# Two attention and feed-forward layers for one new token: one wo load turned on chip, split layer norm, queries turned in PSUM, an earlier gate, and one more V head kept

## The chip, the cores and the metric

The kernel runs on one core of a Trainium2 chip. A core has five engines that run their own queues of instructions side by side: TensorE (PE; its weight loads are shown apart as PEld), VectorE (DVE), ScalarE (ACT), GpSimd (POOL) and SyncE (SP), which here does little but issue loads. Loads from HBM are moved by 16 DMA engines, in the order in which SP issued them. On-chip data lies in SBUF (128 partitions), results of TensorE in PSUM (128 partitions, eight banks of 512 fp32 a partition). The metric is device time in microseconds, lower is better.

## The reference

Four tokens (B = 4), each with its own cache. Two layers share one set of weights and one cache: attention, feed-forward, attention, feed-forward, each with a layer norm in front and a residual sum behind.

```python
def _layernorm(x, axis=-1, eps=1e-5):
    m = jnp.mean(x, axis=axis, keepdims=True)
    v = jnp.var(x, axis=axis, keepdims=True)
    return (x - m) / jnp.sqrt(v + eps)
# x (4,1,512); k_cache, v_cache (4,8,4096,128); wq (512,4096); wo (4096,512); all bf16
def _A_ref(x, k_cache, v_cache, wq, wo):                # 32 query heads, 8 K/V heads, 4096 keys
    q = (x @ wq).reshape(B, Sq, 32, 128).transpose(0, 2, 1, 3)
    k, v = jnp.repeat(k_cache, 4, axis=1), jnp.repeat(v_cache, 4, axis=1)
    scores = jnp.einsum("bhqd,bhkd->bhqk", q, k) * (128 ** -0.5)
    o = jnp.einsum("bhqk,bhkd->bhqd", _softmax(scores), v)
    return o.transpose(0, 2, 1, 3).reshape(B, Sq, 4096) @ wo
def _B_ref(x, w_gate, w_up, w_down):                    # w_gate, w_up (512,1792), w_down (1792,512)
    return (gelu_tanh(x @ w_gate) * (x @ w_up)) @ w_down
x = x + _A_ref(_layernorm(x), ...); x = x + _B_ref(_layernorm(x), ...)
x = x + _A_ref(_layernorm(x), ...); x = x + _B_ref(_layernorm(x), ...)
```

## The kernel before

**Stages.** The kernel goes through the batch one element (token) at a time; "batch 0" to "batch 3" are these four. For each it does the first layer's attention, the first feed-forward and the second layer's attention. The second feed-forward is done once for all four tokens at the end. The first queries of all four tokens are computed at the start (tag "i"), the second queries batch by batch.

**Loads.** All weights stay in SBUF: wq and wo with 32 KB a partition, w_gate, w_up and w_down with 14 KB each. K and V heads of 1 MB (8 KB a partition) go into twelve slots, the tile `KV`. Eight slots hold the K heads of the current batch until the second layer's scores have read them. V turns over in the rest, and is read from HBM twice, once for each layer. `HELD[b]` (line 22) names V heads that stay in their slot from the first layer to the second and so are loaded once: none in batch 0, head 7 in the others. The second layer's V of batches 0 to 2 (`HALVES`) comes in two loads of 512 KB with 4 KB rows, into one half of a slot each. At the end the first four V heads of the second layer of batch 3 go into wq's space, once the last query products have read it.

SP issues, in this order: wq; K of batch 0; the first half of wo; V of batch 0; the second half of wo; w_gate, w_up, w_down in two halves; then for b = 1 to 3: K of batch b, V of batch b for the first layer, V of batch b - 1 for the second; last V of batch 3 for the second layer. Each issue waits on SP until the slot that it overwrites has been read, and everything behind it waits too. `ld_wo` (L794) loads wo with the 128 rows of a head on the partitions, as the products want it, in pieces of 1 KB.

**Order.** The instruction order is not written out. `Plan` (L65) holds a node for each step with an engine, a guessed duration and what it depends on; `Plan.run` lays the nodes out by a small model of the engines and of the DMA, gives each load its slot, and so fixes the order on every engine before the program is built. `LEAD`, `PATIENCE` and the `DMA_` constants (L28 to L41) steer it. `Plan.warm` fills waits of TensorE with idle products (`spin`, L1004).

**Scores.** Six of eight K heads are turned by VectorE (`turn`, L366, in place), two (5 and 7) by TensorE and ScalarE (L373, L379). `scores` (L401) needs the queries spread over the partitions: `qsplit` (L595), `qrep` (L605), `expand` (L392), in two halves z = 0 and z = 1 for K heads 0 to 3 and 4 to 7. Then maximum (L421 to L432), exponential (L438), a turn of the weights (L447 by VectorE, L455 by TensorE, L463 by ScalarE), the products with V (`values`, L485) and the scaling (L493).

**The chain between the attentions.** Output products with wo (`proj`, `proj_last`, L613 and L623), turned and added to the residual (`addback`, L646 and L647). Layer norm: squares (L500), one TensorE product that sums values and squares over the partitions (L506), sums (L512), subtraction of the mean (L513), variance (L521, L522), root by ScalarE (L529, L530); the root is applied later, in the gate or as the scale of the scores. Feed-forward: products with w_gate and w_up into two PSUM banks (L655), each turned by VectorE (`ffturn`, L662), then the gate (L678 to L707), then products with w_down in two halves (L715). The gate's two turned halves share one place in SBUF, so the second turn comes after the first one's use; in `gelu_y` and `gelu_c` the turned up half is multiplied in first, then the reciprocal is taken. Second queries (`qproj`, L829): products with wq for z = 0 and 1 (`qmm`, L538), each copied to bf16 by ScalarE (L551), turned by VectorE (L556) and spread; `qnat` (L563) makes the form that the heads turned by TensorE need.

Of the kernel before, what the change touches and what calls it, by code (L numbers as in the profile page):

```python
# [14 lines left out]
P = 128  # L15
# [6 lines left out]
HELD = ((), (7,), (7,), (7,))  # L22
HALVES = {(b, 1, j) for b in range(3) for j in range(8)} | {(3, 1, 6)}
# [7 lines left out]
DMA_FETCH = 1.5  # L31
DMA_LEAD = 4.0

PATIENCE = (0.5, 1.5, 0.7)
LEAD = {"tn1": -3, "val0": 1, "sc10": -2, "chain": 2, "sc11": -6, "sm00": 1, "os0": -6, "op": -2, "sm01": 11, "sm10": 10, "qx1": 4, "other": 5, "sc00": 2, "sm11": 8, "os1": -4, "tn0": -2, "sc01": 1}
# [3 lines left out]
FILL = 0.7  # L39
SPIN = 0.22  # L40
STREAM = {"sc": 0.85, "qm": 0.85, "up": 0.75, "up2": 0.75, "kt": 0.21, "pw": 0.16, "qp": 0.11, "qn": 0.05,  # L41
          "su": 0.02, "lnm": 0.03, "xt": 0.1, "ys": 0.2, "dn": 0.38, "dn2": 0.38}


def stage(n):
# [13 lines left out]
    if n[0] in ("lnq", "lnm", "lnc", "lnv", "lnr", "up", "ft", "ga", "gb", "gy", "gc", "zz", "dn", "da", "qm", "qe",  # L59
                "qt", "qn", "qc", "qk"):  # L60
        return "chain"
# [3 lines left out]
class Plan:  # L65
# [149 lines left out]
    def warm(self, places):  # L215
# [3 lines left out]
        for n, _ in self.order:  # L219
# [16 lines left out]
            past.append((z, last, 0.72 * d if kind == "val" else d - 0.15 if kind in ("op", "op2") else STREAM.get(kind, 0.0)))  # L236
# [4 lines left out]
def kernel(  # L241
# [261 lines left out]
    def ln_mm(bs, nb):  # L503
        def emit():
            st = R_ps[1][:, 0:2 * CD * nb].rearrange("p (s k b) -> p s k b", s=2, k=CD)
            nc.tensor.matmul(st, lhsT=ones_mean, rhs=XS[:, :, :, bs], start=True, stop=True)  # L506
        return emit

    def ln_mid(bs, nb):
        def emit():  # L510
            st = R_ps[1][:, 0:2 * CD * nb].rearrange("p (s k b) -> p s b k", s=2, k=CD)
            nc.vector.tensor_reduce(out=mu[:, :, 0:nb], in_=st, axis=AX.X, op=ALU.add)  # L512
            nc.vector.tensor_tensor(out=xn[:, :, bs], in0=XT[:, :, bs],  # L513
                                    in1=mu[:, 0, 0:nb].unsqueeze(1).broadcast_to([P, CD, nb]),
                                    op=ALU.subtract)
        return emit

    def ln_var(nb):
        def emit():
            t = lt[:, 0:nb]  # L520
# [12 lines left out]
    def qmm(z, bs, nb):  # L533
# [7 lines left out]
        return emit  # L541

# [46 lines left out]
    def qsplit(z, b):  # L589
        def emit():  # L590
            if b:
# [17 lines left out]
    def proj(src, nb, heads, first, last):  # L609
        def emit():  # L610
            for j in heads:
                for i in range(4):
                    nc.tensor.matmul(R_ps[0][32 * i:32 * i + nb, :], lhsT=src[:, 4 * j + i, 0:nb],  # L613
# [4 lines left out]
    def proj_last(src, nb, heads, last):  # L618
        def emit():
            todo = [4 * j + i for j in heads for i in range(4)]  # L620
            for h in todo:
                for t in range(4):
                    nc.tensor.matmul(R_ps[1][32 * t:32 * t + nb, 0:P], lhsT=src[:, h, 0:nb],  # L623
# [36 lines left out]
    def ffturn(z):  # L660
        def emit():
            nc.vector.transpose(out=PD[:, 0:FT].rearrange("p (c x) -> p c x", c=CF),  # L662
                                in_=R_ps[z][:, 0:FT].rearrange("p (r c) -> p c r", c=CF))
        return emit

    def ff(nb):
        n = CF * nb
        at, ah = (0, n) if nb > 1 else (992, 984)
        d = PD[:, 0:FT].rearrange("p (c x) -> p c x", c=CF)[:, :, 0:nb]
        u = PD[:, FT:FT + n].rearrange("p (c b) -> p c b", c=CF)  # L670
        g = PF[:, at:at + n].rearrange("p (c b) -> p c b", c=CF)
# [19 lines left out]
    def gelu_y(nb, y):  # L691
        def emit():
            d, g, u, h = ff(nb)
            if nb == 1:
                nc.vector.scalar_tensor_tensor(out=g, in0=g, scalar=y, in1=d, op0=ALU.mult, op1=ALU.mult)
            else:
                nc.vector.tensor_tensor(out=g, in0=g, in1=y.unsqueeze(1).broadcast_to([P, CF, nb]),
                                        op=ALU.mult)
                nc.vector.tensor_tensor(out=g, in0=g, in1=d, op=ALU.mult)
        return emit  # L700

    def gelu_c(nb):
# [349 lines left out]
```

## Time and profile before

| | us |
|---|---|
| three runs | 294.04, 294.3, 291.69 (median 294.04) |
| the profiled execution | 291.89 |
| its span in the profile | 290.1 |

The profile shows one execution. DMA moved 111.42 MB from HBM, 97.5 MB of it in 1 MB and 0.5 MB loads of K and V heads. Times in the profile are microseconds from the start of the span. "L715" is line 715 of the kernel before. Views used below: the page (engine shares, the span in 40 slices, the chain of waits that ended last, groups of instructions), windows (one row a stretch: busy time of each engine with its count of instructions, the granted clock of TensorE, the mean busy share of the DMA engines, GB/s), the timeline (instructions in order of time), and the chain of waits in order of time (start, length, what).

### The profile page before, as it was taken

The numbers are of one execution on the slowest core, as the hardware profiler recorded it, in microseconds if no ns is written. First come the engines' busy times: TensorE is split into PE (matmuls) and PEld (weight loads), VectorE is DVE, ScalarE is ACT, GpSimd is POOL, SyncE is SP. The second block draws the span as 40 slices with busy tenths as digits, with TensorE's granted clock in tenths as the row PEclk, the third lists the DMA queues.
The fourth block names the chain that finished last, engine by engine and source line by source line (L and its number), as shares of the span: only waits on it lengthen the run. The fifth ranks groups of instructions, "written<-read, shape, count | busy, mean of one in ns | idle before, by whom it ended". The sixth has DMA issues, their size and how long they took to land.

```text
span 290.1 us, 9733 instructions
## 1 busy us (share of the span) xinstructions
PE 236.3 (81%) x4419; PEld 138.3 (48%) x4419; DVE 133.5 (46%) x380; ACT 74.5 (26%) x167; POOL 0.7 (0%) x6
## 2 busy tenths in 40 slices
PE   4988887878687888798888698879977889897794
PEld 1433454443233565455434465554445655565552
DVE  4149911002289942052389721343998213444034
ACT  1020751001023852101224731000338321113010
POOL 0000000000000000000000000000000000000000
PEclk9999999999999999999999999999999999999999
DMA  7999999999999999999999999999999999999910
GB/s 312 412 421 419 376 405 416 414 371 426 415 407 395 419 421 417 402 407 406 393 417 416 425 416 411 405 407 390 413 422 416 408 387 403 396 382 420 411 47 1
DMA packets 21657, 112.04 MB, mean 386 GB/s; under 512 B 2032, under 2 KB 6128, under 8 KB 12272
## 3 DMA queue, kind: packets, MB, share of 16 engines
q1 hardware_dynamic: 21568, 111.42, 95.3%
q8 instruction: 34, 0.56, 0.8%
q14 instruction: 7, 0.06, 0.0%
q10 hardware_dynamic: 48, 0.01, 0.0%
HBM read 111.42 MB, written 0.00 MB: 384 GB/s over the span
## 4 chain that ended last, share of the span: by engine, by line
DMA 62%; PE 16%; SPq 11%; DVE 7%; issue 2%; ACT 1%; DVEq 0%
DMA KV<-in_A_v_cache_dram 43%; DMA KV<-in_A_k_cache_dram 8%; SPq L351 7%; PE O_ps L485 7%; DMA wd_sb<-in_B_w_down_dram 6%; DMA wq_sb<-in_A_v_cache_dram 5%; SPq L741 3%; PE S_ps L415 3%; DVE KV L366 2%; PE R_ps L715 1%; PE R_ps L538 1%; DVE PA L662 1%; PE S_ps L1004 1%; PE R_ps L655 1%; DVE sm L421 1%
## 5 line engine op out<-in xcount | busy, mean ns | idle before, releaser
L485 PE MATMUL O_ps<-PA,KV 128*128 128x56 bf16 x1920 | 66.3, 188 | 20.8 <-DMA KV<-in_A_v_cache_dram 17.3
L485 PEld LDWEIGHTS <-KV 128*128 128x128 bf16 x1920 | 57.6, 97 | 40.8 <-DMA KV<-in_A_v_cache_dram 32.4
L1004 PE MATMUL S_ps<-iden_b 128*128 128x512 bf16 x226 | 67.7, 401 | 3.6 <-DVE iden_b L321 3.6
L366 DVE STREAM_TRANSPOSE KV<-KV 128x1024 int32<-128x1024 int32 x48 | 56.5, 1214 | 0.6 <-DMA KV<-in_A_k_cache_dram 0.4
L379 ACT ACTIVATE KV<-R_ps 128x512 bf16<-128x512 f32 x64 | 34.9, 595 | 28.0 <-PE R_ps L373 27.9
L415 PE MATMUL S_ps<-KV,PA 128*32 128x512 bf16 x384 | 35.3, 394 | 2.1 <-DVE KV L366 1.3
L1004 PEld LDWEIGHTS <-iden_b 128*128 128x128 bf16 x227 | 21.9, 107 | 27.6 <-issue 11.7
L373 PE MATMUL R_ps<-iden_b,KV 128*128 128x128 bf16 x256 | 22.1, 219 | 6.3 <-ACT KV L379 3.1
L421 DVE TENSOR_REDUCE sm<-S_ps 128x1 f32<-128x512 f32 x16 | 10.8, 677 | 27.4 <-PE S_ps L415 27.4
L373 PEld LDWEIGHTS <-KV 128*128 128x128 bf16 x256 | 15.8, 97 | 14.8 <-issue 10.2
L415 PEld LDWEIGHTS <-PA 128*32 128x32 bf16 x384 | 11.4, 94 | 13.2 <-issue 4.4
L493 DVE TENSOR_TENSOR OT<-O_ps,XS 128x4 bf16<-128x4 f32 (+1 forms) x12 | 2.0, 164 | 32.9 <-PE O_ps L485 32.9
L415 PE MATMUL S_ps<-KV,QN 128*32 128x512 bf16 x128 | 16.8, 381 | 0.2 <-ACT KV L379 0.2
L438 ACT ACTIVATE PA<-S_ps,sm 128x512 bf16<-128x512 f32 x16 | 11.7, 732 | 20.4 <-DVE sm L432 17.6
L632 ACT ACTIVATE PA<-R_ps 128x256 f32<-128x256 f32 x10 | 3.8, 384 | 46.2 <-PE R_ps L613 41.1
L529 ACT ACTIVATE sm<-sm 128x1 f32<-128x1 f32 (+1 forms) x10 | 2.0, 203 | 52.6 <-DVE sm L522 52.6
L493 DVE TENSOR_TENSOR OT<-O_ps,rdk 128x16 bf16<-128x16 f32 (+3 forms) x18 | 3.1, 170 | 26.7 <-PE O_ps L485 26.7
L463 ACT ACTIVATE PA<-T_ps 128x512 bf16<-128x512 f32 x16 | 9.6, 597 | 13.0 <-PE T_ps L455 11.8
L556 DVE STREAM_TRANSPOSE PA<-PA 128x256 int32<-128x256 int32 x10 | 4.4, 437 | 14.9 <-ACT PA L551 14.2
L613 PE MATMUL R_ps<-wo_sb,OT 128*1 128x512 bf16 (+1 forms) x124 | 8.7, 378 | 2.6 <-DMA wo_sb<-in_A_wo_dram 1.4
L646 DVE STREAM_TRANSPOSE PA<-R_ps 128x128 f32<-128x128 f32 x9 | 2.9, 317 | 16.5 <-PE R_ps L623 10.2
L447 DVE STREAM_TRANSPOSE PA<-PA 128x256 int32<-128x256 int32 x16 | 7.0, 434 | 7.5 <-ACT PA L438 7.5
(92 smaller groups left out, 173.9 us busy)
## 6 DMA issues: line engine op xcount, KB each, us to landing
KV<-in_A_v_cache_dram SPq DMA_DIRECT2D x34, 1024.0 KB, 15.0
KV<-in_A_k_cache_dram SPq DMA_DIRECT2D x32, 1024.0 KB, 13.5
KV<-in_A_v_cache_dram SPq DMA_DIRECT2D x46, 512.0 KB, 7.0
wq_sb<-in_A_wq_dram SPq DMA_DIRECT2D x1, 4096.0 KB, 12.2
wo_sb<-in_A_wo_dram SPq DMA_DIRECT2D x2, 2048.0 KB, 19.5
wq_sb<-in_A_v_cache_dram SPq DMA_DIRECT2D x4, 1024.0 KB
wg_sb<-in_B_w_gate_dram SPq DMA_DIRECT2D x1, 1792.0 KB
wu_sb<-in_B_w_up_dram SPq DMA_DIRECT2D x1, 1792.0 KB
```

Source lines behind the costliest of these rows:

```text
L351: nc.sync.dma_start(out=where[name], in_=src.rearrange("(p c) d -> p (c d)", p=P))
L366: nc.vector.transpose(out=w, in_=w)
L373: nc.tensor.matmul(R_ps[k % 2][:, P * u:P * u + P], lhsT=where[name][:, at:at + P], rhs=iden_b[:], start=True, stop=True)
L379: nc.scalar.activation(out=where[name][:, 512 * k:512 * k + 512], in_=R_ps[k % 2][:], func=ACT.Copy)
L415: nc.tensor.matmul(S_ps[z][32 * t:32 * t + 32], lhsT=w, rhs=k, start=(m == 0 and x == 0), stop=(m == 1 and x == 3))
L421: nc.vector.tensor_reduce(out=cms[:, z:z + 1], in_=S_ps[z][:].rearrange("p c r -> p (c r)"), axis=AX.X, op=ALU.max)
L438: nc.scalar.activation(out=PW[L][z].rearrange("p (a r e) -> p a r e", a=8, e=2), in_=S_ps[z][:].rearrange("p (a e) r -> p a r e", e=2), fu ...
L463: nc.scalar.activation(out=PW[L][z], in_=T_ps[z][:].rearrange("p t x -> p (t x)"), func=ACT.Copy)
L485: nc.tensor.matmul(Ov[L][:, j], lhsT=vw[:, c, :], rhs=w[:, c // 2, :, c % 2].unsqueeze(1).broadcast_to([P, WIDE, 4]), start=(m == 0 and c ...
L613: nc.tensor.matmul(R_ps[0][32 * i:32 * i + nb, :], lhsT=src[:, 4 * j + i, 0:nb], rhs=wo_sb[:, 4 * j + i, :], start=(first and j == heads[0 ...
L741: return lambda pick: nc.sync.dma_start(out=dst, in_=src.rearrange(pat, q=P))
L1004: nc.tensor.matmul(sinks[place].rearrange("p (a n) -> p a n", a=4), lhsT=iden_b[:], rhs=every, start=True, stop=True)
```

## The change

- wo comes in one load of 4 MB with 32 KB rows, ahead of V of batch 0, with 32 heads on the partitions of each quarter; VectorE turns it in place in eight pieces (`wo_turn`), which puts it into the layout of before. All output products of the first layer wait for all eight.
- Layer norm takes two TensorE products: one for the values, which the subtraction waits for, and one for the squares.
- Second queries, half z = 0: the products leave the query's elements in another order (`qmm_apart`), VectorE turns the whole bank in PSUM in place, and `qsplit` reads it there. ScalarE's copy to bf16 is gone for this half; z = 1 is as before.
- Gate: reciprocal and scale come before the up half is multiplied in (`gelu_d`); the up half is turned and multiplied in two pieces (`ffturn(1, k)`, `gelu_h`), each followed by its half of the w_down products.
- V head 7 of batch 0 is kept for the second layer (`HELD`), so SP has one head, or two half loads, fewer.
- The final feed-forward uses the same code as the others, and the planner's constants are changed.

In the built program SP's list has one wo load in place of two and 14 half loads instead of 16 after the V loads of batch 1; the rest of its order is the same. K head 3 of batch 1 gets a slot that held a K head of batch 0; before, it got one that had held V. TensorE has 4371 products instead of 4373, with 430 idle ones instead of 454.

```diff
-HELD = ((), (7,), (7,), (7,))
-HALVES = {(b, 1, j) for b in range(3) for j in range(8)} | {(3, 1, 6)}
+HELD = ((7,), (7,), (7,), (7,))
+HALVES = {(b, 1, j) for b in range(3) for j in range(7)} | {(3, 1, 6)}
-DMA_FETCH = 1.5
+DMA_FETCH = 0.8
-PATIENCE = (0.5, 1.5, 0.7)
+PATIENCE = (0.5, 1.5, 0.6)
...
-    def ln_mm(bs, nb):
+    def ln_mm(s, bs, nb):
         def emit():
-            st = R_ps[1][:, 0:2 * CD * nb].rearrange("p (s k b) -> p s k b", s=2, k=CD)
-            nc.tensor.matmul(st, lhsT=ones_mean, rhs=XS[:, :, :, bs], start=True, stop=True)
+            st = R_ps[1][:, s * CD * nb:(s + 1) * CD * nb].rearrange("p (k b) -> p k b", k=CD)
+            nc.tensor.matmul(st, lhsT=ones_mean, rhs=XS[:, s, :, bs], start=True, stop=True)
...
+    def qmm_apart(bs):
+        def emit():
+            for c in range(CD):
+                w = wq_sb[:, c, :].rearrange("q (z g h j k e) -> q z g h j e k", z=2, g=2, h=8, j=2, e=2)
+                for jg in range(4):
+                    nc.tensor.matmul(R_ps[0][32 * jg:32 * jg + 1, :].rearrange("p (h e k) -> p h e k", h=8, e=2),
+                                     lhsT=xn[:, c, bs], rhs=w[:, 0, jg % 2, :, jg // 2],
+                                     start=(c == 0), stop=(c == CD - 1))
+        return emit
+
+    def qturn_apart():
+        nc.vector.transpose(out=R_ps[0][:], in_=R_ps[0][:])
...
-    def gelu_c(nb):
+    def gelu_d(nb, y):
         def emit():
             d, g, u, h = ff(nb)
             nc.vector.tensor_scalar(out=u, in0=u, scalar1=1.0, scalar2=1e30, op0=ALU.add, op1=ALU.min)
             nc.vector.reciprocal(out=u, in_=u)
-            nc.vector.tensor_tensor(out=h, in0=g, in1=u, op=ALU.mult)
+            if nb == 1:
+                nc.vector.scalar_tensor_tensor(out=g, in0=g, scalar=y, in1=u, op0=ALU.mult, op1=ALU.mult)
...
+    def gelu_h(nb, k):
+        def emit():
+            d, g, u, h = ff(nb)
+            c = slice(CF // 2 * k, CF // 2 * k + CF // 2)
+            nc.vector.tensor_tensor(out=h[:, c], in0=g[:, c], in1=d[:, c], op=ALU.mult)
...
-    def ld_wo(n):
-        return lambda pick: nc.sync.dma_start(
-            out=wo_sb[:, 16 * n:16 * n + 16],
-            in_=A_wo[2048 * n:2048 * n + 2048].rearrange("(h p) n -> p h n", p=P))
+    def ld_wo(pick):
+        nc.sync.dma_start(out=wo_sb[:].rearrange("p c n -> p (c n)"),
+                          in_=A_wo.rearrange("(h q c) n -> q h (c n)", q=4, c=32))
+
+    def wo_turn(k):
+        def emit():
+            w = wo_sb[:].rearrange("p c n -> p (c n)").bitcast(I32).rearrange("p (c n) -> p n c", c=32)
+            w = w[:, 32 * k:32 * k + 32]
+            nc.vector.transpose(out=w, in_=w)
+        return emit
...
     loads_k(0)
-    pl.load(("wo", 0), 20.5, ld_wo(0), None)
+    pl.load("wo", 31.2, ld_wo, None)
     loads_v(0, 0)
-    pl.load(("wo", 1), 20.5, ld_wo(1), None)
...
+            if not z and not root:
+                after = add(("qm", tag, z), "PE", 1.1, [after], qmm_apart(bs), ins=32)
+                last = add(("qt", tag, z), "DVE", 0.72, [after], qturn_apart)
+                last = spread_q(b, 1, z, last, "apart")
+                continue
...
+    wo_ready = [add(("wt", k), "DVE", 2.16, ["wo"], wo_turn(k)) for k in range(8)]
...
-            return [(h, [("os", b, 0, i), ("wo", h[0] // 4)]) for i, h in enumerate(g)]
+            return [(h, [("os", b, 0, i)] + wo_ready) for i, h in enumerate(g)]
...
+        e = add(("gd", tag), "DVE", 0.65 if one else 0.95, [e], gelu_d(nb, y))
+        t1, h, n = a, None, None
+        for k in range(2):
+            t1 = add(("ft", tag, 1 + k), "DVE", 0.37, [g[1], t1], ffturn(1, k))
+            h = add(("gh", tag, k), "DVE", 0.15, [t1, e, h], gelu_h(nb, k))
+            if k and clear:
+                add(("zz", tag), "DVE", 0.07, [h], clear)
+            n = add(("dn", tag, k), "PE", 0.48, [h, n, ("wd", k)], down(nb, k), ins=56)
```

More of the change, by code (lines that the diff above doesn't have):

```diff
@@ L607, in qrep, with proj @@
         return emit
-    def proj(src, nb, heads, first, last):
+    def proj(src, cols, nb, heads, first, last):
         def emit():
@@ L616, in proj, with proj_last @@
         return emit
-    def proj_last(src, nb, heads, last):
+    def proj_last(src, cols, nb, heads, last):
         def emit():
```

144 lines of the change are left out of this document (67 added, 77 removed).

## The prediction

> **What bounds the kernel now.** I read the page first: engine shares, the DMA row, the chain of waits.
>
> ```profile
> span 290.1 us, 9733 instructions
> PE 236.3 (81%) x4419; PEld 138.3 (48%) x4419; DVE 133.5 (46%) x380; ACT 74.5 (26%) x167; POOL 0.7 (0%) x6
> DMA  7999999999999999999999999999999999999910
> q1 hardware_dynamic: 21568, 111.42, 95.3%
> DMA 62%; PE 16%; SPq 11%; DVE 7%; issue 2%; ACT 1%; DVEq 0%
> ```
>
> The DMA engines are busy in every slice but the last two, and the chain of work that ended last is mostly DMA. TensorE's 81% holds filler products (L1004) and is no bound. So a microsecond counts if it shortens the byte stream, closes a hole in it, or lies in the tail behind the last byte. The view by windows shows where the stream is thinner than its normal rate (last column GB/s; the column before it the busy share):
>
> ```profile
> 14.00:30.00 16.00, 13.87 (x127) 5.74 (x126) 11.61 (x16) 1.63 (x4) 0.00 (x0) 1.00 1.01 421
> 30.00:42.00 12.00, 10.05 (x130) 5.75 (x121) 5.82 (x12) 9.76 (x19) 0.00 (x0) 1.00 1.05 383
> 56.00:68.00 12.00, 8.95 (x110) 4.07 (x108) 0.49 (x3) 0.77 (x2) 0.00 (x0) 1.00 1.06 387
> 86.50:90.00 3.50, 2.64 (x51) 1.55 (x51) 3.07 (x13) 1.18 (x4) 0.00 (x0) 1.00 0.88 346
> 120.00:138.00 18.00, 15.86 (x398) 10.38 (x394) 6.64 (x31) 2.01 (x7) 0.00 (x0) 1.00 1.03 407
> 138.00:152.00 14.00, 11.89 (x186) 5.86 (x185) 8.56 (x22) 3.11 (x8) 0.00 (x0) 1.00 1.01 404
> 198.00:212.00 14.00, 11.98 (x182) 5.75 (x178) 9.28 (x24) 3.21 (x8) 0.00 (x0) 1.00 1.01 408
> 228.00:242.00 14.00, 11.97 (x276) 8.18 (x273) 2.49 (x10) 3.23 (x7) 0.00 (x0) 1.00 0.99 390
> 254.00:258.00 4.00, 3.54 (x68) 1.66 (x60) 1.11 (x3) 0.60 (x1) 0.00 (x0) 1.00 1.00 346
> 276.00:278.00 2.00, 1.95 (x53) 1.21 (x50) 0.18 (x1) 0.03 (x1) 0.00 (x0) 1.00 0.28 104
> ```
>
> K heads in 8 KB rows flow at 421 GB/s, V halves in 4 KB rows at 407. The two wo halves lie in the second and third row. At 86.5 the stream thins, and it ends near 276.5; the granted clock is 1.00 in every row.
>
> **wo in one load.** Both halves move the same bytes as the one load. Against 421, the two 12 us rows lack (421-383)/421 x 12 = 1.08 and (421-387)/421 x 12 = 0.97 us, together 2.0. Does a load in 32 KB rows run at full rate? wq is such a load:
>
> ```profile
> wq_sb<-in_A_wq_dram SPq DMA_DIRECT2D x1, 4096.0 KB, 12.2
> ```
>
> 4.19 MB in 12.2 us from issue is 10.0 us at 421 GB/s plus 2.2 us of latency, so yes. Term: **-2.0**, ends -1.0 (only one row's lack is wo's doing) and -2.2. [...]
>
> The second half also moves ahead of the eight V loads on SP's queue, so those land about 4 us later. Nothing pays: the layer's end waits for w_down, behind the same bytes as before.
>
> **Turning wo.** Eight VectorE turns of 128x1024 words, element step 1 KB. The nearest rows:
>
> ```profile
> L366 DVE STREAM_TRANSPOSE KV<-KV 128x1024 int32<-128x1024 int32 x48 | 56.5, 1214 | 0.6 <-DMA KV<-in_A_k_cache_dram 0.4 <-issue 0.2
> L662 DVE STREAM_TRANSPOSE PA<-R_ps 128x448 f32<-128x448 f32 x10 | 6.5, 648 | 7.2 <-PE R_ps L655 7.1
> L646 DVE STREAM_TRANSPOSE PA<-R_ps 128x128 f32<-128x128 f32 x9 | 2.9, 317 | 16.5 <-PE R_ps L623 10.2 <-PE R_ps L715 6.3
> L728 DVE STREAM_TRANSPOSE PA<-PA 128x128 f32<-128x128 f32 x1 | 0.4, 408 | 0.0
> ```
>
> and, from the chain, the load of V head 3 of batch 0 (start, length):
>
> ```profile
> 35.23 14.77 DMA KV<-in_A_v_cache_dram
> ```
>
> L646 and L662 give (648-317)/320 = 1.03 ns an element and 0.19 us fixed. L728 writes with a step: (408-185)/128 = 1.74 ns. So a turn is 1.2 us (contiguous, L366) to 2.0 (0.19 + 1024 x 1.74 ns); I take 2.0, the row with a step. Head 3 landed at 50.0; four V loads of 2.5 us and a wo half of 6 before that, the last K load ended near 34. So the one wo load lands about 44, and the turns end by 44 + 16 + 1.5 of other VectorE work = 61.5. Behind the first turn stands the turn of the weights of V heads 4 to 7 (L447), whose first V lands about 50.0 + 2.5 + 4 = 56.5; that wait is covered. The output products wait for all turns, but V head 7 lands only near 64 (50.0 + 10 + 4). Cost 0; without that cover 16 us.
>
> **V head 7 kept.** It saves one load of two halves: 1.049 MB / 407 GB/s = 2.58 us. But it keeps one of the four slots in which V turns over, and the fourth K load of batch 1 took that slot. SP's rows (start, duration, count):
>
> ```profile
> 61.62 1.33 SPq L351 DMA_DIRECT2D KV<-in_A_k_cache_dram  x3
> 65.98 21.25 SPq L351 DMA_DIRECT2D KV<-in_A_k_cache_dram  x3
> 86.42 2.58 SPq L351 DMA_DIRECT2D KV<-in_A_k_cache_dram  x3
> ```
>
> Three K loads went at 61.62, the fourth at 65.98, the fifth at 86.42, when the second layer's scores of batch 0 had freed the first K slots. In the changed order the fourth waits for those scores too, and every later load stands behind it on SP. Now the stream runs thin just when the fifth is issued (346 GB/s, a loss of (421-346)/421 x 3.5 = 0.6 us). Changed, the bytes in hand end 2.0 (wo) + 2.5 (a K head, 1.049 MB / 421) = 4.5 us earlier, while the scores come only about 2 us earlier (next part). The hole grows by some 2.5 us. Put the other way: from the scores on, the stream has one K head more (+2.49) and one V head less (-2.58). Keeping the head is worth **-0.1**, not -2.6; the ends are -2.6 (no hole) and +0.5.
>
> **The chain up to those scores.** It starts when w_down lands; chain of waits, and the one VectorE row from the timeline:
>
> ```profile
> 61.10 17.76 DMA wd_sb<-in_B_w_down_dram
> 78.90 0.59 PE R_ps L715 x28
> 80.07 0.18 DVE XS L500
> 80.29 0.40 PE R_ps L506 x2
> 80.71 0.18 DVE sm L512
> 80.91 0.17 DVE xn L513
> 81.16 1.04 PE R_ps L538 x16
> 82.22 0.61 ACT PA L551
> 82.85 0.46 DVE PA L556
> 83.33 0.27 DVE qs L595
> 81.38 1.25 DVE L366 STREAM_TRANSPOSE KV<-KV 128x1024 int32<-128x1024 int32 x1
> ```
>
> The squares (0.18 plus a hop) leave the path: the query products start at 80.94 on this clock, not 81.16. The second product (0.40, as L506) runs while VectorE sums and subtracts (0.18 + 0.17 and hops); without that cover it would cost its 0.40. ScalarE's copy and the turn (82.22 to 83.31) become one turn of 128x512 in PSUM: 0.19 + 512 x 1.03 ns = 0.72 us, possible from 82.0. But in the changed VectorE order the K turn (81.38 to 82.63) stands ahead of it; before, ScalarE's copy hid that turn. So it ends at 82.65 + 0.72 = 83.37, against 83.31: **+0.1**, ends -0.6 (K turn out of the way) and +0.4 (a turn that writes PSUM at L728's 1.74 ns: 1.08). In batches 1 to 3 the order has the query turn first, and the chain there is shorter by 0.2 + 0.2 (two norms) and 0.4 (82.22 to 83.31 is 1.09, less 0.72).
>
> **Later holes.** The stage of batch 1 ran at 404 (138 to 152), the same stage of batch 2, which already keeps a head, at 408: 4/419 x 14 = 0.13, term **-0.15**. Batch 3 lacks (407-390)/407 x 14 = 0.58 at 228 to 242 and (407-346)/407 x 4 = 0.60 at 254 to 258, where the first V loads into wq's space wait for the last query products. A chain shorter by 0.8 us should close some: **-0.5**, ends 0 and -1.2.
>
> **The tail.**
>
> ```profile
> 280.68 0.17 DVE XS L500
> 281.81 0.96 PE R_ps L655 x16
> 282.79 0.66 DVE PA L662
> 285.31 0.52 DVE PA L706
> 286.12 0.98 PE R_ps L715 x56
> ```
>
> The squares leave the path here too (-0.2). In the gate, the reciprocal runs before the second turn, which is halved (0.19 + 224 x 1.03 ns = 0.42 each); the down products' first half starts after one half turn, but two half turns cost 0.84 instead of 0.66, so I count nothing for it. Term **-0.2**, ends 0 and -0.5.
>
> **Sum**: -2.0 - 0.1 + 0.1 - 0.15 - 0.5 - 0.2 = -2.85. The profiled execution took 291.89 (1.8 around its span), so it becomes 289.0. The shown runs are 294.04, 294.3 and 291.69; with the profiled one their mean is 292.98. I take the change off that mean: **290.1**.
>
> **Rivals.**
>
> *The kept head is not given back* (0.25). The hole stays as small as now, because the scores come earlier or the transfers in hand last longer. For it: the fifth K load was issued just as the stream thinned, so the stage is near balance, and 0.6 us hang on one K turn. Against: bytes in hand shrink by a whole head. It gives up to -2.85 - 2.5, about 287.6.
>
> *Only wo counts* (0.16): batch 3's holes stay, and the query turn is at its long end. Then -2.85 + 0.5 + 0.3 + 0.15 and some of wo's term, about -1.5: 291.5.
>
> *wo is turned too late* (0.09), the case on the slower side. All output products wait for eight turns. From there to the down products are some 7 us (an estimate: 280.68 to 286.12 in the tail's rows is 5.4, and the products, half sums and turn ahead of it), and w_down lands at about 78.9 - 2.0 = 77; so turns that end past 70 move the chain, the scores and the stream behind them. The point is (70 - 45.5)/8 = 3.1 us a turn. At 4 us the turns end at 77.5 and the end moves by +7.5, net +4.6: 297.6. [...] That the change does not do what it says is no case: SP's order has one wo load and two half loads fewer.
>
> The forecast's own case has 0.50. About 1% (2.9 us) is what a measurement can tell from no change, and the forecast lies on that edge, so I halve it: faster 0.25 + 0.25 = 0.50; same 0.25 + 0.16 = 0.41; slower 0.09. The range goes from the first rival against the profiled execution (291.89 - 5.3 = 286.6) to a gain of 1.3 against the highest run shown (294.3 - 1.3 = 293.0), about where the second rival ends.
>
> **What would show it.** Right: 30 to 42 near 420 GB/s and no second thin stretch at 56 to 68; the fourth K load issued near 84.5; a stretch of 2 to 4 us before 87 well under 346 GB/s; wo turns near 2.0 us, done before V head 7 lands. A full stream through 80 to 90 would make the first rival true; output products of batch 0 waiting on a wo turn, the third. If the last byte lands near 274 (276.5 less 2.65) and some 13.4 us follow it (13.6 now), the sum held.

## The result and the profile after

| | kernel before | changed kernel |
|---|---|---|
| median of the runs, us | 293.38 | 360.3 (357.81 to 362.0) |
| ratio, 95% interval | | 1.228 [1.218, 1.238] |
| profiled execution, us | 291.89 | 357.81 |
| its span, us | 290.1 | 356.0 |

The change makes the kernel 67 us slower by the medians; the forecast was 290.1 us, a gain. (Where a ratio below does not match its medians, single disturbed runs are left out of the ratio. And one count of the section on the change is wrong: idle products went from 227 to 215; 454 and 430 counted their weight loads too.)

The page of the changed kernel, in the order of the lines shown of before: engine shares, the granted clock, the DMA engines' busy share and GB/s in 40 slices of 8.9 us, the queue's share, the chain that ended last, and the group of wo's turns.

```profile
span 356.0 us, 9762 instructions
PE 236.0 (66%) x4427; PEld 142.1 (40%) x4427; DVE 153.4 (43%) x408; ACT 72.2 (20%) x163; POOL 0.7 (0%) x6
PEclk9999875555555999999999999999999999999999
DMA  8999993222223999699999999999999999999940
GB/s 354 390 421 339 199 176 67 52 59 66 55 59 105 352 435 414 272 392 417 419 409 406 396 415 422 417 414 388 372 370 418 418 418 417 406 338 413 422 168 1
q1 hardware_dynamic: 17284, 110.37, 81.6%
DMA 51%; PE 19%; another core or an unknown queue 18%; DVE 6%; ACT 2%; issue 1%; SPq 1%; DVEq 0%; ACTq 0%
L824 DVE STREAM_TRANSPOSE wo_sb<-wo_sb 128x1024 int32<-128x1024 int32 x8 | 16.9, 2180 | 64.9 <-DMA wo_sb<-in_A_wo_dram 64.9
```

Before, every slice but the first and the last two was full. Now seven slices in a row have a DMA share of two or three tenths, six of them with 52 to 67 GB/s. TensorE has as much work as before (236.0 us), spread over a longer span; its granted clock falls to half while it stands (0.50 from 60 to 108). VectorE waits 64.9 us for wo, once. The queue's share fell too (81.6% against 95.3%): the engines were idle, not busy with something new. The same stretch by windows (the columns before the last two are the granted clock and, from the right, GB/s and DMA share):

```profile
14.00:30.00 16.00, 13.62 (x130) 5.53 (x129) 13.08 (x19) 1.96 (x5) 0.00 (x0) 1.00 1.01 421
30.00:42.00 12.00, 8.81 (x96) 5.14 (x95) 4.52 (x9) 8.59 (x18) 0.00 (x0) 0.86 1.07 243
60.00:64.00 4.00, 0.00 (x0) 0.00 (x0) 0.00 (x0) 0.00 (x0) 0.00 (x0) 0.50 0.26 57
64.00:108.00 44.00, 0.00 (x0) 0.00 (x0) 0.00 (x0) 0.00 (x0) 0.00 (x0) 0.50 0.25 58
148.00:152.00 4.00, 3.24 (x62) 1.47 (x66) 3.57 (x8) 0.18 (x1) 0.00 (x0) 1.00 0.34 88
```

From 64 to 108 nothing computes, and the DMA share is 0.25: four of sixteen engines. They move 58 GB/s, 14.5 each; at 421 GB/s each of sixteen moves 26.3. In the trace's records of DMA packets, wo's 128 rows of 32 KB run from 31.85 to 109.68, 78 us, four at a time; a row takes 2.43 us at the median, where a row of wq takes 1.21. SP's own rows (start, duration, count) show what stood behind it:

```profile
15.36 0.71 SPq L817 DMA_DIRECT2D wo_sb<-in_A_wo_dram  x1
17.85 103.69 SPq L351 DMA_DIRECT2D KV<-in_A_v_cache_dram  x8
```

Before, the row of the V loads was:

```profile
17.88 33.57 SPq L351 DMA_DIRECT2D KV<-in_A_v_cache_dram  x8
```

The chain of the changed kernel:

```profile
47.13 65.49 another core or an unknown queue
112.67 1.67 PE O_ps L485 x32
123.25 19.84 DMA wd_sb<-in_B_w_down_dram
```

wo is issued in its place, at 15.36. The first four V loads were issued right behind; they are spread over all sixteen engines, and on the four that wo holds their shares wait until it is through: by the landing records, twelve of the sixteen shares of each V load land between 38 and 57 us, the other four between 110 and 120. So V head 0 is there at 112.6, and SP, which waits for a free slot before the fifth V load, needs 103.69 us for eight issues, where it needed 33.57. w_down stands behind them on SP. It lands at 123.25 + 19.84 = 143.09, where before it was 61.10 + 17.76 = 78.86: 64.2 of the 65.9 us are lost by then. From there to the end it is 356.0 - 143.09 = 212.9, before 290.1 - 78.86 = 211.2. The rest of the change gained nothing either.

### The profile page after: what moved, and what is told of

It reads as the page before. It is cut to its first block, busy times and chain, and to the rows that moved or that the text cites. A ratio compares the mean times of both kernels' runs of the same rounds, so it can differ in the third digit from the quotient of the medians.

```text
span 356.0 us, 9762 instructions
## 1 busy us (share of the span) xinstructions
PE 236.0 (66%) x4427; PEld 142.1 (40%) x4427; DVE 153.4 (43%) x408; ACT 72.2 (20%) x163; POOL 0.7 (0%) x6
## 3 DMA queue, kind: packets, MB, share of 16 engines
q1 hardware_dynamic: 17284, 110.37, 81.6%
## 4 chain that ended last, share of the span: by engine, by line
DMA 51%; PE 19%; another core or an unknown queue 18%; DVE 6%; ACT 2%; issue 1%; SPq 1%; DVEq 0%; ACTq 0%
DMA KV<-in_A_v_cache_dram 27%; DMA KV<-in_A_k_cache_dram 11%; PE O_ps L485 8%; DMA wd_sb<-in_B_w_down_dram 6%; DMA wq_sb<-in_A_v_cache_dram 4%; DMA wq_sb<-in_A_wq_dram 3%; PE S_ps L415 3%; PE S_ps L1038 2%; PE R_ps L675 2%; ACT PA L438 1%; PE R_ps L737 1%; DVE KV L366 1%; PE R_ps L506 1%; DVE sm L421 1%
## 5 line engine op out<-in xcount | busy, mean ns | idle before, releaser
L485 PE MATMUL O_ps<-PA,KV 128*128 128x56 bf16 x1920 | 67.3, 190 | 82.4 <-DMA KV<-in_A_v_cache_dram 81.1
L485 PEld LDWEIGHTS <-KV 128*128 128x128 bf16 x1920 | 58.7, 98 | 103.0 <-DMA KV<-in_A_v_cache_dram 93.3
L1038 PE MATMUL S_ps<-iden_b 128*128 128x512 bf16 x214 | 62.0, 392 | 3.6 <-DVE iden_b L321 3.6
L824 DVE STREAM_TRANSPOSE wo_sb<-wo_sb 128x1024 int32<-128x1024 int32 x8 | 16.9, 2180 | 64.9 <-DMA wo_sb<-in_A_wo_dram 64.9
L415 PE MATMUL S_ps<-KV,PA 128*32 128x512 bf16 x384 | 36.8, 398 | 2.3 <-DVE KV L366 1.0
L1038 PEld LDWEIGHTS <-iden_b 128*128 128x128 bf16 x215 | 20.4, 105 | 25.3 <-issue 8.3
L373 PE MATMUL R_ps<-iden_b,KV 128*128 128x128 bf16 x256 | 23.0, 223 | 8.3 <-DMA KV<-in_A_k_cache_dram 4.7
L373 PEld LDWEIGHTS <-KV 128*128 128x128 bf16 x256 | 16.2, 99 | 15.9 <-issue 8.7
L415 PEld LDWEIGHTS <-PA 128*32 128x32 bf16 x384 | 12.2, 95 | 13.5 <-issue 5.9
L438 ACT ACTIVATE PA<-S_ps,sm 128x512 bf16<-128x512 f32 x16 | 11.7, 733 | 25.9 <-DVE sm L432 25.6
L468 PE MATMUL S_ps<-mask_th,sm 128*128 128x16 f32 x32 | 6.1, 267 | 5.2 <-ACT PA L438 5.1
L684 DVE STREAM_TRANSPOSE PA<-R_ps 128x224 f32<-128x224 f32 (+1 forms) x15 | 7.4, 490 | 5.1 <-PE R_ps L675 4.8
```

Of the source, the lines that this page charges most:

```text
L373: nc.tensor.matmul(R_ps[k % 2][:, P * u:P * u + P], lhsT=where[name][:, at:at + P], rhs=iden_b[:], start=True, stop=True)
L415: nc.tensor.matmul(S_ps[z][32 * t:32 * t + 32], lhsT=w, rhs=k, start=(m == 0 and x == 0), stop=(m == 1 and x == 3))
L438: nc.scalar.activation(out=PW[L][z].rearrange("p (a r e) -> p a r e", a=8, e=2), in_=S_ps[z][:].rearrange("p (a e) r -> p a r e", e=2), fu ...
L485: nc.tensor.matmul(Ov[L][:, j], lhsT=vw[:, c, :], rhs=w[:, c // 2, :, c % 2].unsqueeze(1).broadcast_to([P, WIDE, 4]), start=(m == 0 and c ...
L684: nc.vector.transpose(out=PD[:, 32 * c0:32 * c1].rearrange("p (c x) -> p c x", x=32), in_=R_ps[z][:, 0:FT].rearrange("p (r c) -> p c r", c ...
L824: nc.vector.transpose(out=w, in_=w)
```

## The experiments: which part costs

**All of the change but wo.** wo is loaded as before and not turned.

```diff
-    pl.load("wo", 31.2, ld_wo, None)
+    pl.load(("wo", 0), 20.5, ld_wo(0), None)
     loads_v(0, 0)
+    pl.load(("wo", 1), 20.5, ld_wo(1), None)
...
-    wo_ready = [add(("wt", k), "DVE", 2.16, ["wo"], wo_turn(k)) for k in range(8)]
```

> The changed kernel with wo loaded as before (two halves in 1 KB rows, no turn); all else of the change stays. Theory S (the one wo load is split by its outermost source step, which counts four, so 4 of 16 DMA engines carry it): the 66 us go, and the rest of the change does what the prediction's other terms say, -0.85 us: 291 to 293, against 293.4 before. Theory L (rows of 32 KB that lie 128 KB apart are slow as such, on any number of engines): the same here. Theory R (the kept head, the split norm, the query turn in PSUM or the new order cost time by themselves): 300 or more.

Measured: 295.23 against 292.63, ratio 1.0084 [1.0053, 1.0116]. The great loss is gone, but the rest is not the small gain that theory S had.

**wo alone.** The kernel before with the one load and the turns, all else as it was (the same two places, the other way round).

> The kernel before with wo's one load and its eight turns alone. Theories S and L: all of the loss, 355 to 364. Theory R: under 350, since other parts carry some of it.

Measured, in one execution: 359.97, VectorE waiting 68.3 us for wo:

```profile
L802 DVE STREAM_TRANSPOSE wo_sb<-wo_sb 128x1024 int32<-128x1024 int32 x8 | 16.8, 2202 | 68.3 <-DMA wo_sb<-in_A_wo_dram 68.3
```

The two together put the whole loss on wo's load with its turns; the next run, which keeps the turns, separates these two. They also show that the rest, which I had at -0.85, costs 2.5 us (ratio 1.0084).

## The experiments: why the load is slow

The load's source is the pattern [4][32][16384]: four quarters of a head's rows, 32 heads, 32 KB; its destination is 128 partitions. wq's source is [128][16384].

**The same rows in four loads**, one for each quarter, so that the outermost count of each is 32.

```diff
-        nc.sync.dma_start(out=wo_sb[:].rearrange("p c n -> p (c n)"),
-                          in_=A_wo.rearrange("(h q c) n -> q h (c n)", q=4, c=32))
+        return lambda pick: nc.sync.dma_start(
+            out=wo_sb[32 * q:32 * q + 32].rearrange("p c n -> p (c n)"),
+            in_=A_wo.rearrange("(h q c) n -> q h (c n)", q=4, c=32)[q])
```

> The changed kernel with wo in four loads, one for each quarter of the partitions; the same 32 KB rows, 128 KB apart, the same turns, but each load's outermost step counts 32. Theory S: each load spreads over 16 engines; wo takes 10 us at full rate, 20 if a quarter of the partitions takes data at only half of it, and the kernel takes 290 to 302. Theory L: wo stays near 78 us and the kernel near 358.

Measured: 304.82, ratio 1.0416 [1.0372, 1.046], a little above the 302 of theory S. Windows of this kernel:

```profile
30.00:34.00 4.00, 3.44 (x45) 2.13 (x45) 3.96 (x9) 4.00 (x10) 0.00 (x0) 1.00 1.22 367
38.00:42.00 4.00, 3.88 (x33) 1.98 (x33) 0.00 (x0) 2.17 (x5) 0.00 (x0) 0.57 0.95 201
42.00:46.00 4.00, 3.27 (x26) 1.10 (x24) 1.28 (x5) 1.32 (x4) 0.00 (x0) 1.00 0.94 197
```

Rows, their size and their distance in HBM are those of the one load, and the stall is gone: all engines are busy (0.94, 0.95). So it is the number of engines. But these loads into 32 partitions ran at half the 421 GB/s, 197 to 201 (a row takes 2.55 us at the median, on sixteen engines), and 304.82 is 9.6 us above the kernel with wo as before (295.23). The turns are not what costs that: the output products start behind them at 72.8, and w_down lands at 67.42 + 19.95 = 87.37, where with wo as before it lands at 79.12.

**An outermost count of two** (64 rows in each part; wo's rows then stand in another order than the products need).

```diff
-                          in_=A_wo.rearrange("(h q c) n -> q h (c n)", q=4, c=32))
+                          in_=A_wo.rearrange("(b a c) n -> a b (c n)", a=2, c=32))
```

> The changed kernel, but the one wo load takes its rows in another order, so that its outermost source step counts two (64 rows of 32 KB each, 64 KB apart); wo's rows lie in the wrong places, so the output isn't the reference's. Theory S: 2 of 16 DMA engines carry it, so alone it keeps the DMA busy share near 0.13. How long it takes tells what held the four back, which took about 76 us for 128 rows, 2.4 us a row, and wq's 32 KB rows take half of that on 16 engines. If the four were slowed by each other (they step through the four quarters of the partitions side by side), two engines that work far apart run at full speed: 64 rows of 1.2 us, again 76 to 80 us, and the kernel 355 to 365. If a single engine is slow with such rows by itself: 155 us and a kernel of 430 to 440. Theory L with no split: share as in the changed kernel, 0.25.

Measured, in one execution: 367.41, a little more than the 355 to 365 expected for two engines at full speed. Windows:

```profile
64.00:108.00 44.00, 0.00 (x0) 0.00 (x0) 0.00 (x0) 0.00 (x0) 0.00 (x0) 0.50 0.23 71
100.00:112.00 12.00, 0.00 (x0) 0.00 (x0) 0.00 (x0) 0.00 (x0) 0.00 (x0) 0.50 0.13 55
```

When only wo is left (100 to 112), the share is 0.13, two of sixteen, and two engines move 55 GB/s, 27.5 each: as fast as an engine of a full load (26.3), and together about as fast as the four of the changed kernel. A row takes 1.21 us at the median, as for wq. So a single engine is not slow with such rows; each of the four moved half as much, 14.5.

**The four quarters on two queues**, SP's and ScalarE's.

```diff
+        return lambda pick: (nc.sync if q < 2 else nc.scalar).dma_start(
```

> As the run with four quarter loads, but quarters 0 and 1 are issued by SP and 2 and 3 by ScalarE's queue, so that two quarters are under way at once. If a quarter of the partitions takes data at half the full rate and two quarters don't disturb each other, wo moves at 400 GB/s or more and the kernel comes to 293 to 296, like the run with wo loaded as before less its 2 us. If the DMA engines take the two queues' rows one after the other at the same slow rate: 303 to 306, as with one queue.

Measured: 306.33, ratio 1.0464 [1.0421, 1.0506]; over one queue 304.82. Rows of the timeline show when the quarters were issued:

```profile
9.58 3.64 ACTq L817 DMA_DIRECT2D wo_sb<-in_A_wo_dram  x2
29.54 2.82 SPq L817 DMA_DIRECT2D wo_sb<-in_A_wo_dram  x2
```

The kernel did not do what the run was made for. ScalarE's two quarters went out 20 us ahead of SP's: their packets run from 12.9 to 24.6 us, those of SP's two from 42.2 to 55.7. No two quarters on different queues were ever under way at once, so what two at once would give stays open. ScalarE's rows took 2.28 us at the median, SP's 2.56: slow on either queue.

The engines' busy share went with the outermost count of the load's source: 0.25 for 4 (the changed kernel), 0.13 for 2, 0.94 and 0.95 for 32, and 0.92 to 0.94 for wq's 128 (from 4 to 12 us, before). Four engines at 26.3 GB/s would need 40 us (an estimate: 4.19 MB at 4 x 26.3), and it took 78. That the four slowed one another is my reading of the 14.5 GB/s of each beside the 27.5 of each of the two. What halved the rate of the four, and that of the sixteen that wrote 32 partitions (197 to 201 and not 421), no run shows.

## The experiments: the rest of the change

**Without the kept head** (wo as before, nothing kept for batch 0).

```diff
-HELD = ((7,), (7,), (7,), (7,))
+HELD = ((), (7,), (7,), (7,))
```

> As the run with wo loaded as before, and V head 7 of batch 0 isn't kept either: one more load of 1 MB. The prediction's step (the head is given back by a longer hole ahead of the fourth K load of batch 1): within 0.5 us of the run that keeps it. The first rival (the kept head is a clear gain): 2.0 to 2.6 us slower than it.

Measured: 296.08, ratio 1.0122 [1.0078, 1.0166]. By the medians the head is worth 0.85 us in this order, between the two expectations; the intervals overlap.

**With the planner's constants of before** (wo as before).

```diff
-DMA_FETCH = 0.8
+DMA_FETCH = 1.5
-PATIENCE = (0.5, 1.5, 0.6)
+PATIENCE = (0.5, 1.5, 0.7)
```

> The run with wo loaded as before, with the planner's constants of before as well (PATIENCE, LEAD, DMA_FETCH, FILL and the loads' sizes). Theory P (the 2.6 us by which that run is slower than the kernel before come from the order and from too few idle products, which let TensorE's granted clock fall to half four times): no such falls, and 291 to 293. Theory Q (the new steps themselves or the kept head cost them): 294 to 297.

Measured: 297.27, ratio 1.0157 [1.0114, 1.02]. The new constants are not the cause; with the old ones it is no faster.

**More idle products** (wo as before).

```diff
-WARM = 0.45
+WARM = 0.6
```

> The run with wo loaded as before, with more idle products (248 instead of 225: the planner's WARM at 0.6 instead of 0.45). If the four falls of the granted clock cost the time: fewer of them and 1 to 3 us less, 292 to 294. If they are hidden beside the DMA: no change within 0.6 us, 295.

Measured: 296.35, ratio 1.0111 [1.0066, 1.0155]. In the profiled execution (296.67) the clock is 1.00 from 84 to 252 us, where the kernel without the added products has four stretches of 3.4 us at half clock; it is not faster for that. (From 252 to 262 it is 0.83.) The falls of the clock alone don't explain the loss.

**Each part alone on the kernel before**, with its lines of the change's diff: the kept head (`HELD`, `HALVES`), the norm (`ln_mm`, its two sums, `ln`), the query turn (`qmm_apart`, `qturn_apart`), the gate (`gelu_d`, `gelu_h`, `ffturn(1, k)`). In the norm's and in the query turn's part, the query products of z = 1 also wait for the variance. The shortest and the norm's:

```diff
-HELD = ((), (7,), (7,), (7,))
+HELD = ((7,), (7,), (7,), (7,))
```

```diff
-        a = add(("lnm", tag), "PE", 0.4, [a], ln_mm(bs, nb), ins=4)
+        m = add(("lnm", tag), "PE", 0.35, [after], ln_mm(0, bs, nb), ins=4)
+        a = add(("lnc", tag), "DVE", 0.3, [m], ln_mid(bs, nb))
+        s = add(("lns", tag), "PE", 0.35, [s, m], ln_mm(1, bs, nb), ins=4)
```

> The kernel before, in which only V head 7 of batch 0 is kept. The rest of the change without wo cost 2.5 us (295.23 against 292.63), and taking the kept head out of it cost another 0.85. Theory K, the kept head is worth about the same in the order of before: 1 us less than before, some 291.6, with a hole near 86 us in which the fourth K load of batch 1 waits for the scores of the second layer. Theory P of the prediction: -0.1, no difference. Rival, the head costs time in the order of before because nothing of the chain is shorter there: 1 to 2 us more than before.

> The kernel before, in which only layer norm takes two TensorE products. Theory of the prediction: the chain between the attentions is shorter by 0.2 twice in each batch and the end by 0.2: 0.2 to 0.7 us less than before. Rival N, the product of the squares stands ahead of the query products on TensorE, or its sum on VectorE ahead of the chain, and costs its 0.4: up to 2 us more than before, over eight norms.

> The kernel before, in which only half z = 0 of the second queries is turned in PSUM. Theory of the prediction: +0.1 in batch 0, about -0.4 in each of the others, of which some shows: 0 to 1 us less than before. Rival T, the part that costs the 3.3 us that the change without wo and without the kept head lacks: the turn of 0.72 us waits on VectorE behind K turns of 1.2 us, where ScalarE's copy ran beside them, and the scores, the K slots and the loads behind them come later: 1 to 3 us more than before.

> The kernel before, in which only the gate's reciprocal comes first and the up half is turned and multiplied in two pieces. Theory of the prediction: nothing in the tail, within 0.5 us of before. Rival G, the part that costs: two turns of 0.42 instead of one of 0.66 and one more product on VectorE in each gate make each chain longer by some 0.3 to 0.5 us, and K turns get between the pieces: 1 to 3 us more than before.

| part alone | median (before 293.11) | ratio |
|---|---|---|
| head kept | 292.66 | 0.998 [0.9961, 1.0] |
| norm in two products | 294.72 | 1.0031 [1.0003, 1.006] |
| query turn | 292.65 | 0.9975 [0.9946, 1.0004] |
| gate | 293.18 | 1.0004 [0.9973, 1.0035] |

Summed they are -0.3 us, not +2.5: either they do not add, or one costs more in company. So parts were put together, by the same lines.

> The kernel before with all of the change except wo, the layer norm and the planner's constants: head kept, query turn, gate. Alone they measured 0.998, 0.9975 and 1.0004 of the kernel before, together 0.996 if they add: 292.0 where before is 293.1. Theory N, the layer norm in two products is what makes the whole slower: 292 to 292.5. Rival A, any two or three of these parts together disturb the order, and nothing adds: 294 to 296, near the 295.23 of the change without wo.

> The kernel before with the kept head and the query turn alone, the two parts that measured below it (0.998 and 0.9975). If they add, 0.9955 of before, 291.8 where it is 293.1: the best version of the study. Rival A, they disturb each other: 293 to 295.

> The kernel before with the kept head and the layer norm in two products, alone 0.998 and 1.0031. If they add: 1.001, about 293.4. If the loss of 2.5 us in the change without wo comes from the norm meeting the kept head (fewer bytes in hand where the clock falls and the value products free the slots late): 295 to 296.5.

> The kernel before with the layer norm in two products and the query turn, alone 1.0031 and 0.9975. If they add: 1.0006, about 293.3. If the loss comes from the norm meeting the query turn (the chain made shorter twice, so that the second layer's scores and products come while VectorE and TensorE still work on the next K heads): 295 to 297, as in the change without wo and without the kept head (296.08).

| parts, constants of before | median (before 293.0) | ratio |
|---|---|---|
| head, query, gate | 293.23 | 1.0013 [0.999, 1.0035] |
| head, query | 292.73 | 0.9984 [0.9969, 0.9998] |
| head, norm | 296.75 | 1.0109 [1.008, 1.0139] |
| norm, query | 294.76 | 1.0068 [1.0043, 1.0093] |

Every version with the norm is slower than before, none without it is by more than 0.13%: that is what points at the norm. Its price depends on its company. Alone it is 0.31%, 0.9 us; beside the query turn 0.68 + 0.25 = 0.93%, 2.7 us; beside the kept head 1.09 + 0.20 = 1.29%, 3.8 us. (The run with the planner's constants of before, at 1.57%, has all four parts but also the changed form of the final feed-forward, so its 1.44% above head, query and gate is not the norm's alone.) Head, query and gate together came out between their two expectations. Head and query turn together are 0.5 us below before (0.9984), where the two ratios alone would multiply to 0.9955; the intervals overlap, so whether they add is open, and no version gained more than 0.25%.

The timelines say what the norm does. First the kernel before: residual sum, squares, product, sum, difference, first feed-forward product.

```profile
69.27 0.17 DVE L647 TENSOR_TENSOR XS<-XS,PA 128x4 f32<-128x4 f32 x1
69.47 0.17 DVE L500 TENSOR_TENSOR XS<-XS 128x4 f32<-128x4 f32 x1
69.69 0.39 PE L506 MATMUL R_ps<-XS,sm 128*128 128x8 f32 x2 [0.56 <-DVE XS L500]
70.12 0.17 DVE L512 TENSOR_REDUCE sm<-R_ps 128x2 f32<-128x8 f32 x1 [0.48 <-PE R_ps L506]
70.54 0.93 PE L655 MATMUL R_ps<-wg_sb,xn 128*1 128x448 bf16 x16
```

Then the kernel with head and norm (its profiled execution took 297.7), the same place, and its norm ahead of the second queries of batch 2:

```profile
69.31 0.17 DVE L651 TENSOR_TENSOR XS<-XS,PA 128x4 f32<-128x4 f32 x1
69.53 0.61 PE L506 MATMUL R_ps<-XS,sm 128*128 128x4 f32 x4 [0.36 <-DVE XS L651]
70.18 0.16 DVE L511 TENSOR_REDUCE sm<-R_ps 128x1 f32<-128x4 f32 x1 [0.50 <-PE R_ps L506]
70.60 0.74 PE L659 MATMUL R_ps<-wg_sb,xn 128*1 128x448 bf16 x12 [0.46 <-DVE sm L511]
...
195.74 0.39 PE L506 MATMUL R_ps<-XS,sm 128*128 128x4 f32 x2
196.72 1.03 PE L542 MATMUL R_ps<-wq_sb,xn 128*1 128x512 bf16 x16
197.69 0.44 PE L485 MATMUL O_ps<-PA,KV 128*128 128x56 bf16 x10
199.46 0.32 PE L485 MATMUL O_ps<-PA,KV 128*128 128x56 bf16 x6 [1.33 <-issue]
199.62 0.36 PE L506 MATMUL R_ps<-XS,sm 128*128 128x4 f32 x2
204.39 1.03 PE L542 MATMUL R_ps<-wq_sb,xn 128*1 128x512 bf16 x16
```

Where the two products stand together, the sum of the values starts only after both: from residual sum to the first product it takes 1.29 us, before 1.27. The squares leave the path, and the second product takes their place. Where the planner puts products with V between them, the second one comes 3.9 us after the first (199.62 and 195.74, and likewise 138.63 and 134.70), behind an issue gap of 1.33 in them (time in which TensorE waited for nothing that the profile shows), and variance, root and the query products of z = 1 come behind that. The wait of z = 1 for the variance is not enough by itself: the query turn alone has it too, and was not slower.

The stream shows where this kernel loses. Against the kernel with the kept head alone it moves 386 and not 406 GB/s from 120 to 150 us, 379 and not 403 from 180 to 210, and 392 and not 409 from 240 to 270, the stretches with the second queries of batches 1 to 3; between these the two agree within 5 GB/s. That is (20 + 24 + 17)/421 x 30 = 4.3 of the 5.4 us between the two spans. A rival stays. Issue gaps of that size stand in other kernels too, but late: 1.21 at 262.15 before, 0.94 at 255.22 and 1.20 at 261.41 with the head alone. With head and norm they fall into the second queries of batches 1 and 2 (1.38 and 1.33). Whether the late product costs the time or the gap that falls there, these runs don't separate.

Two runs asked how much that lateness costs: the two products kept together in one step (on head, query and gate), and the old single product issued twice.

```diff
-        a = add(("lnm", tag), "PE", 0.4, [a], ln_mm(bs, nb), ins=4)
+        m = add(("lnm", tag), "PE", 0.6, [after, s], ln_mms(bs, nb), ins=8)
```

```diff
+            for _ in range(2):
+                nc.tensor.matmul(st, lhsT=ones_mean, rhs=XS[:, :, :, bs], start=True, stop=True)
```

> Head kept, query turn, gate (293.23 where before is 293.0), and the layer norm in two products that stand one right behind the other on TensorE, where the planner is not free to put products with V between them. Theory L, the norm costs because its second product waits on TensorE behind V products (138.63 behind 134.70, 199.62 behind 195.74 in the kernel with kept head and norm), and the variance, the products of z = 1 and the exponential come late: with the two together the loss is gone, 292.8 to 294, though nothing is gained either, since the sum of the values then waits for both products (0.61 us instead of 0.39). Rival S, the added wait of z = 1 for the variance, or the order that any longer norm gives, is enough: 295 to 297.5, as with the norm free (297.27).

> Head kept, query turn, gate, with the single product of each layer norm issued twice, the order otherwise unchanged: the same time on TensorE (0.6 us instead of 0.4) and the same shift of all later instructions, without a second step that can be moved. Theory L: 0 to 0.6 us more than 293.23. Rival S, that any shift of TensorE's instructions by a few places moves its fetch stalls and its clock and costs 2 to 4 us: 295 to 297.

Measured against 293.02: together 295.43, ratio 1.0075 [1.0043, 1.0106]; twice 294.95, ratio 1.0056 [1.0024, 1.0088]. Theory L missed both times: with the two together the loss is not gone, and the product issued twice costs more than 0.6 us. Rival S met its range in the first run and stayed just under it in the second. Above the same kernel with the old norm (1.0013), the product issued twice costs 0.43%, 1.3 us, and the two kept together 0.62%, 1.8 us. So a norm that is only longer on TensorE costs time without any late product, though for the product issued twice the difference is hardly clear of the noise. The two left free cost up to 3.8 us, but that was measured beside the head alone, so what the lateness adds to those 1.3 to 1.8 us is not measured. The intervals of the two runs overlap, and whether their share is the 0.2 us that each of two norms a batch adds to the chain, or the moved places of what follows, stays open.

## Why the prediction was wrong

**wo in one load: the step that failed.** "Does a load in 32 KB rows run at full rate? wq is such a load", and "so yes". wq was the nearest row by the size of its rows, and I compared nothing else. The loads differ in the outermost count of the source, 128 and 4. The term was -2.0 with ends -1.0 and -2.2; measured it is +65 (360.3 against 295.23 without it) to +67 (359.97 against 292.63 alone). No end and no rival held a load on four engines. Whether wo in large rows gains the 2.0 us at full rate was not measured: every load tried was slow in another way.

**Turning wo: right in size, at another time.** 2.18 us a turn against 2.0 taken; below the 3.1 us from which the third rival decides. The turns were late because the load was: they ran from 110.3 to 127.4, and the output products behind them from 128.54. Even so that rival's path is not where the time went: the up products at 138.78 still waited for w_up, and the down products at 140.96 for w_down. The way to the loss was another: V's shares on four engines, the slots of V, SP's queue, w_down. My sentence that V lands about 4 us later and "nothing pays" took the queue behind wo to be delayed by wo's bytes alone. V head 3 landed at 120.1, before at 50.0.

**V head 7 kept: the mechanism right, the gain under-sized.** The hole is there. Windows of the kernel with only this part, then of before:

```profile
82.00:88.00 6.00, 5.50 (x83) 2.27 (x75) 5.32 (x10) 1.39 (x4) 0.00 (x0) 1.00 0.63 217
```

```profile
82.00:88.00 6.00, 5.45 (x79) 2.31 (x72) 5.32 (x12) 1.37 (x3) 0.00 (x0) 1.00 0.94 385
```

217 against 385 GB/s over 6 us is (385 - 217)/421 x 6 = 2.4 us, where I had "some 2.5". The fourth K load goes at 86.61 and lands at 91.30; before, the fifth one landed at 92.10. So a K head less has come by then and a V head less is left, as I put it, but the K head costs less than the 2.49 us that I took: the fifth is there at 93.79, 1.7 us later than before. Less the 2.58 us of V that is -0.9. The term was -0.1; alone it measured -0.6 us [-1.1, 0], within its ends. The first rival, a head not given back (-2.5), is refuted.

**The chain to the scores.** The turn in PSUM took 0.72 us (0.72 taken), a half turn of the gate 0.411 (0.42). With the change but for wo, batch 0 takes from the down products to the second layer's first scores 84.54 - 79.16 = 5.38 us, before 84.39 - 78.90 = 5.49: -0.1 where I had +0.1, inside the ends. The K turn does stand ahead of the query turn (81.64 to 82.89), as I had it, so what the squares save could not have shown here anyway; that the term comes out near is in part luck. The query turn alone gave -0.7 us [-1.6, +0.1]. The squares "leave the path" was wrong, since the second product took their place: 1.29 against 1.27 us. I let it run "while VectorE sums and subtracts"; the sum waits for both products.

**Later holes and tail: not found.** Windows with all of the change but wo, then before:

```profile
188.00:196.00 8.00, 7.39 (x203) 4.79 (x203) 4.71 (x24) 0.62 (x3) 0.00 (x0) 1.00 0.94 355
252.00:260.00 8.00, 7.27 (x183) 4.53 (x172) 3.19 (x15) 1.00 (x3) 0.00 (x0) 1.00 1.01 381
```

```profile
188.00:196.00 8.00, 6.24 (x186) 4.47 (x187) 3.63 (x19) 0.62 (x3) 0.00 (x0) 1.00 1.03 407
252.00:260.00 8.00, 7.52 (x181) 4.60 (x178) 2.67 (x8) 1.78 (x5) 0.00 (x0) 1.00 1.03 382
```

Batch 3's hole did not close (381 and 382), and batch 2's stage got a new one: (407 - 355)/407 x 8 = 1.0 us. -0.5 and -0.15 became a loss. The last V half landed 12.3 us before the end of the span (281.29 of 293.5), before 11.7 (278.44 of 290.1): the tail's -0.2 is not there. For all of these I counted what the norm takes off the chain, and nothing for the second product: neither its own time ahead of the sum nor where it would stand in TensorE's queue.

## What to carry to other kernels

Before a load is costed by the size of its rows, write down the outermost count of its source. Here rows of 32 KB with a count of 4 moved on four engines (share 0.25), with 2 on two (0.13), with 32 on all sixteen (0.94 to 0.95), and a DMA share of a quarter in one window shows it at once. The load on four engines also held up the shares of the V loads behind it on those engines (they landed at 110 to 120 us, the others at 38 to 57), so its price was paid by what was queued behind: w_down came 64.2 us later. And a step that is split to take work off a path must be costed with its second half: where that half stands in its engine's queue, and what now waits for it.

## What the hardware showed that I had not expected

- One load of 4 MB ran on four engines at 57 to 58 GB/s, and on two at 55: each of two engines moved 27.5, each of four 14.5, and a row of 32 KB took 1.21 and 2.43 us.
- 16 engines that wrote wo's rows into 32 partitions at a time moved 197 to 201 GB/s, half of the 421 of K heads into 128 partitions.
- Behind the load on four engines, twelve of the sixteen shares of each of the next four V loads landed between 38 and 57 us, the other four between 110 and 120.
- VectorE turned 128x1024 words with a step of 1 KB in 2.18 us, contiguous ones in 1.21: 1.8 times as long.
- TensorE's granted clock stood at 0.50 while it had nothing to do (64 to 108), and was 1.00 again at 148.
